# One attention-and-experts kernel: from hand-written loops to one list of small operations, with other load shapes for q, k and v

## The chip, the cores and the metric

The kernel runs on one core of a Trainium2 chip. The metric is the device time of one execution in microseconds (us), median over several runs. The core has five instruction queues that run side by side and meet only at semaphores: TensorE (PE, with weight loads shown as PEld), VectorE (DVE), ScalarE (ACT), GpSimd (POOL) and SyncE (SP, which here only issues DMA transfers). Each queue runs its instructions strictly in the order in which the program lists them.

## The reference, cut to what matters

```python
B, H, S, D = 8, 8, 576, 64            # batch, heads, tokens, head size
scores = q @ k.T / sqrt(D)            # per batch and head
scores = where(|i - j| <= 32, scores, -1e9)
x = softmax(scores) @ v               # -> 4608 tokens x 512
logits = x @ w_gate + modality_bias[modality_id]     # 8 experts
e = argmax(logits); g = max(softmax(logits))
out[token] = g * (relu(x[token] @ w1[e]) @ w2[e])    # w1 512x1024, w2 1024x512
```

Sliding-window attention gives one row of 512 values per token; each row goes to the one expert that its gate chooses.

## The kernel before

**Attention.** A batch has four pairs of heads, so there are 32 pairs (the loop variable `it`). q and k are loaded for four heads at a time with four tokens to a partition (packets of 1,024 bytes, `load_main`); the last 64 tokens of all heads come in a transfer of their own (`load_rest`, 256-byte packets), and v comes with one token to a partition (`load_v`, 256-byte packets). POOL casts all of it to bf16 (`pool_cast`, L110). PE transposes q and k (L212, L222), DVE and ACT copy the results out (L213, L214, L227, L225), PE makes scores of a 192-wide window (L238), ACT exponentiates (L242, L245), DVE multiplies by the band mask (L250), PE multiplies by v with a column of ones (L261, L266), and DVE divides (L271, L272).

**Routing.** After a batch's four pairs its rows are transposed (L349, L351) and multiplied by the gate (L360). Some 25 small DVE operations (`best`, `place`, `dispatch`) choose the expert and the row's place in a scratch table in DRAM; POOL scatters the rows there (L435).

**Experts.** The table is worked off in 19 tiles of 256 tokens. A tile is gathered by SP (L463), transposed (`turn`, L475 and L478), multiplied by w1 in four pieces (`up`, L490, relu on ACT at L492) and by w2 in two halves of two pieces each (`down`, L499), scaled on DVE (L503) and scattered to the output by POOL (L506). Two tiles per batch go to the two experts that are expected to be the fullest, with weights loaded once at the start (`load_ab`); the three tiles of `tail` may load other weights.

**What sets the order.** Two loops. The loop over `it` issues the stages of pairs `it`, `it+1` and `it+2`, loads of batch b+2 and casts of batch b+1. `trickle(n)` puts a few of the routing steps of the batch before into the gaps, `work(n)` a piece of a tile. After the last pair eight pairs' worth of loop steps are left, and `tail` follows. Nothing but this order decides what stands behind what in each queue. There is one PSUM buffer for `up` (tag "h"), one for `down` ("y"), one for scores ("s"), one for values ("o"), and two for all transposes ("tp").

Of the kernel before, what the change touches and what calls it, by code (L numbers as in the profile page):

```python
# [29 lines left out]

@with_exitstack
def kernel(
# [12 lines left out]
    nc = tc.nc  # L45
# [9 lines left out]
    R = 4  # L55
    SM = P * R
    SR = S - SM
# [18 lines left out]
    ld = ctx.enter_context(tc.tile_pool(name="ld", bufs=8))  # L76
    ldv = ctx.enter_context(tc.tile_pool(name="ldv", bufs=2))
    ldr = ctx.enter_context(tc.tile_pool(name="ldr", bufs=2))
# [15 lines left out]
    scr_ins = []  # L94

# [13 lines left out]
    def pool_cast(o_ap, i_ap):  # L109
        nc.gpsimd.tensor_scalar(out=o_ap, in0=i_ap, scalar1=1.0, scalar2=0.0, op0=ALU.mult, op1=ALU.add)  # L110


    Ld = {}

    def load_main(b, g):
        for u, src in ((0, q), (1, k)):
            f_ = ld.tile([P, 4, R * D], FP32, tag="qkf", name="qkf")
            nc.sync.dma_start(
                f_[:], src[b, 4 * g:4 * g + 4, 0:SM, :].rearrange("h (p r) d -> p h (r d)", r=R))
            Ld[b, g, u] = f_  # L120

    def load_rest(b):
        rf = ldr.tile([P, H, D], FP32, tag="rf", name="rf")
        nc.sync.dma_start(rf[0:SR], q[b, :, SM:S, :].rearrange("h s d -> s h d"))
        nc.sync.dma_start(rf[SR:P], k[b, :, SM:S, :].rearrange("h s d -> s h d"))
        Ld[b, "r"] = rf

    def load_v(b, eng):
        f_ = ldv.tile([P, NM - 1, H, D], FP32, tag="vf", name="vf")
        l_ = ldv.tile([SR, H, D], FP32, tag="vl", name="vl")  # L130
        for j in range(NM - 1):
            eng.dma_start(f_[:, j], v[b, :, P * j:P * j + P, :].rearrange("h s d -> s h d"))
        eng.dma_start(l_[:], v[b, :, SM:S, :].rearrange("h s d -> s h d"))
        Ld[b, "v"] = f_, l_
# [3 lines left out]
    def cast_main(b, g, split=False):  # L138
        for u in range(2):
            c_ = ldb.tile([P, R, 4 * D], BF16, tag=f"cb{u}", name="cb")  # L140
            o_ap = c_[:].rearrange("p r (h d) -> p h r d", h=4)
            i_ap = Ld[b, g, u][:].rearrange("p h (r d) -> p h r d", r=R)
            (nc.scalar.copy if split and u else pool_cast)(o_ap, i_ap)
            Ct[b, g, u] = c_

    def cast_rest(b):
        rb = ldr.tile([P, HD], BF16, tag="rb", name="rb")
        pool_cast(rb[:], Ld[b, "r"][:].rearrange("p h d -> p (h d)"))
        Ct[b, "r"] = rb

    def cast_v(b, i):
        f_, l_ = Ld[b, "v"]
        if i < 2:
            pool_cast(v_t[b % 2][:, 2 * i:2 * i + 2, :, 0:D].rearrange("p j h d -> p (j h) d"),
                      f_[:, 2 * i:2 * i + 2].rearrange("p j h d -> p (j h) d"))
        else:
            pool_cast(v_t[b % 2][0:SR, NM - 1, :, 0:D], l_[:])

    load_main(0, 0)
    load_rest(0)  # L160

    mb_bc = const.tile([P, n_mod, E], FP32)
    nc.scalar.dma_start(mb_bc[:], moe_modality_bias.partition_broadcast(P))
    mid64 = const.tile([NM * B, P], mybir.dt.int64)
    nc.vector.memset(mid64[:].bitcast(I32), 0)
    idv = moe_modality_id.rearrange("(b s) -> b s", s=S)
    for m in range(NM):
# [4 lines left out]
    load_v(0, nc.scalar)  # L172
    load_main(0, 1)
    ident = const.tile([P, P], BF16)
    make_identity(nc, ident[:])


# [9 lines left out]
    mask = const.tile([P, WIN], BF16)  # L187
    nc.gpsimd.memset(mask[:], 1.0)
    nc.gpsimd.affine_select(out=mask[:], in_=mask[:], compare_op=ALU.is_ge, fill=0.0,
                            base=0, pattern=[[1, WIN]], channel_multiplier=-1)  # L190
    nc.gpsimd.affine_select(out=mask[:], in_=mask[:], compare_op=ALU.is_ge, fill=0.0,
                            base=64, pattern=[[-1, WIN]], channel_multiplier=1)

    def prep(i):
        nc.vector.memset(q_t[i][:, :, 0:QP], 0.0)
        nc.vector.memset(q_t[i][:, :, QP + S:], 0.0)
        nc.vector.memset(k_t[i][:, :, S:], 0.0)
        pv = p_t[i][:].rearrange("p h (j c) -> p h j c", c=SW)
        nc.vector.memset(pv[:, :, :, WL:SW], 0.0)
        nc.vector.memset(v_t[i][:, 0:NM - 1, :, D:D + 1], 1.0)  # L200
        nc.vector.memset(v_t[i][0:SR, NM - 1, :, D:D + 1], 1.0)
        nc.vector.memset(v_t[i][SR:P, NM - 1], 0.0)
        nc.vector.memset(x_t[i][:, :, HD // 2 + 2:ROW // 2], 0)
    prep(0)
    cast_main(0, 0, split=True)
    cast_rest(0)


    def tr_rest(b):
        tpr = ps_t.tile([P, NH, P], BF16, tag="tp", name="tpr")  # L210
        for hp in range(NH):
            nc.tensor.transpose(tpr[:, hp, :], Ct[b, "r"][:, P * hp:P * hp + P], ident[:])  # L212
        nc.vector.tensor_copy(q_t[b % 2][:, :, QP + SM:QP + S], tpr[:, :, 0:SR])  # L213
        nc.vector.tensor_copy(k_t[b % 2][:, :, SM:S], tpr[:, :, SR:P])  # L214

    def tr_main(it):
        b, hp = divmod(it, NH)
        g, l = hp // 2, 2 * (hp % 2)
        for u in (1, 0):
            tp = ps_t.tile([P, R, P], BF16, tag="tp", name=f"tp{u}")  # L220
            for i in range(R):
                nc.tensor.transpose(tp[:, i, :], Ct[b, g, u][:, i, D * l:D * l + P], ident[:])  # L222
            i_ap = tp[:].rearrange("d r c -> d c r")
            if u:
                nc.scalar.copy(k_t[b % 2][:, hp, 0:SM].rearrange("d (c r) -> d c r", r=R), i_ap)  # L225
            else:
                nc.vector.tensor_copy(q_t[b % 2][:, hp, QP:QP + SM].rearrange("d (c r) -> d c r", r=R), i_ap)  # L227

    def scores(it, j0, st=None):
        b, hp = divmod(it, NH)  # L230
        pt = p_t[it % 2]
        if st is None:
            st = ps_s.tile([P, 2, 512], FP32, tag="s", name="st")
        for j in (j0, j0 + 1) + ((4,) if j0 else ()):
            c0 = WIN * (j - j0)
            w_ = WIN if j < NM - 1 else WL
            for h in range(2):
                nc.tensor.matmul(  # L238
                    st[:, h, c0:c0 + w_], k_t[b % 2][D * h:D * h + D, hp, P * j:P * j + P],
                    q_t[b % 2][D * h:D * h + D, hp, P * j:P * j + w_], start=True, stop=True)  # L240
        p_ap = pt[:, :, SW * j0:SW * j0 + 2 * SW].rearrange("p h (j c) -> p h j c", c=SW)[:, :, :, 0:WIN]
        nc.scalar.activation(  # L242
            p_ap, st[:, :, 0:2 * WIN].rearrange("p h (j c) -> p h j c", c=WIN), ACT.Exp, scale=scale)
        if j0:
            nc.scalar.activation(pt[:, :, 4 * SW:4 * SW + WL], st[:, :, 2 * WIN:2 * WIN + WL],  # L245
                                 ACT.Exp, scale=scale)

    def masking(it):
        p_ap = p_t[it % 2][:].rearrange("p h (j c) -> p (h j) c", c=SW)[:, :, 0:WIN]
        nc.vector.tensor_tensor(  # L250
            out=p_ap, in0=p_ap, in1=mask[:].unsqueeze(1).to_broadcast([P, 2 * NM, WIN]), op=ALU.mult)

    def values(it):
        b, hp = divmod(it, NH)
        pt, vt = p_t[it % 2], v_t[b % 2]
        xr = x_t[b % 2][:, :, 0:HD // 2].bitcast(BF16)
        ot = ps_o.tile([P, 2, 512], FP32, tag="o", name="ot")
        for h in range(2):
            for m in range(NM):
                o_ap = ot[:, h, (D + 1) * m:(D + 1) * (m + 1)]  # L260
                nc.tensor.matmul(  # L261
                    o_ap, pt[:, h, SW * m:SW * m + P], vt[:, m, 2 * hp + h, :],
                    start=(m == 0), stop=(m == 0), skip_group_check=True)
                if m > 0:
                    c1 = SW * (m - 1) + P
                    nc.tensor.matmul(  # L266
                        o_ap, pt[:, h, c1:c1 + P], vt[:, m - 1, 2 * hp + h, :],
                        start=False, stop=True, skip_group_check=True)
        o_v = ot[:, :, 0:NM * (D + 1)].rearrange("p h (m c) -> p h m c", c=D + 1)
        rec = small.tile([P, 2, NM], FP32, tag="rec", name="rec")  # L270
        nc.vector.reciprocal(rec[:].unsqueeze(3), o_v[:, :, :, D:D + 1])  # L271
        nc.vector.tensor_tensor(  # L272
            out=xr[:, :, P * hp:P * hp + P].rearrange("p m (h d) -> p h m d", h=2),
            in0=o_v[:, :, :, 0:D],
            in1=rec[:].unsqueeze(3).to_broadcast([P, 2, NM, D]), op=ALU.mult)

    cast_v(0, 0)
    cast_v(0, 1)
    cast_v(0, 2)
    load_main(1, 0)  # L280
    load_rest(1)
    load_main(1, 1)
    load_v(1, nc.sync)
    prep(1)


# [468 lines left out]
    def run_all(g):  # L755
        for _ in g:
            pass
# [133 lines left out]
```

## Time and profile before

| | us |
|---|---|
| median of 9 runs | 331.65 (330.55 to 333.26) |
| the profiled execution, as timed | 334.06 |
| its span, first to last instruction | 332.4 |
| values of the first pair divided (L271) | from 36.4 |
| of the 13th pair | from 110.6 |
| of the 32nd pair | from 236.1 |
| the last matmul ends | 315.7 |

Columns of a row of a window are the busy us of each engine in that stretch, with the number of instructions, the granted TensorE clock (1 is full), the mean load of the 16 DMA engines (packets of several queues overlap, so it can be over 1) and the rate. A row of a wait says who idled, which instruction ended it, the sum, how often and the longest. In a timeline the bracket at the end is the idle time before the instruction and what ended it.

### The profile page before, as it was taken

To read this page: it belongs to the slowest core of one execution; us is meant where nothing else is said; L and a number is where in the kernel's file an instruction comes from. 1 tells how busy PE (TensorE), PEld (TensorE's weight loads), DVE (VectorE), ACT (ScalarE), POOL (GpSimd) and SP (SyncE) were. 2 spreads that over 40 slices of the span, in tenths; PEclk is the share of its full clock that TensorE was granted. 3 is DMA by queue.
4 is the path that set the end of the run, shared out by engine and by line. 5 is a ranking of instruction groups with operands and counts; after the bars stand their busy time and mean duration, and the time that the engine had idled before them with its cause. 6 is when DMAs were issued, how large, how long until landed. Compare 5 with 4: busy or idle time off the path is not lost. (4 is left out here: it accounts for less than half of the span.)

```text
span 332.4 us, 6885 instructions
## 1 busy us (share of the span) xinstructions
PE 238.4 (72%) x2587; PEld 166.8 (50%) x2617; DVE 177.3 (53%) x464; ACT 162.3 (49%) x274; POOL 151.3 (46%) x195
## 2 busy tenths in 40 slices
PE   0104766736589989989988998998878799788700
PEld 0003554525466756756765675675655456555300
DVE  4025888833826587687789479657333741111100
ACT  0206575643437856857756765784544233343100
POOL 3159741286280636736837835814517312221310
PEclk9999997655569999999999999999999989999975
DMA  4999999999996952895597511231332764210110
GB/s 144 249 289 251 220 233 214 235 309 259 282 220 188 268 138 75 249 267 157 178 313 190 168 43 43 100 132 53 92 129 97 261 215 130 74 57 1 71 62 1
DMA packets 79351, 55.32 MB, mean 166 GB/s; under 512 B 49192, under 2 KB 74832, under 8 KB 79312
## 3 DMA queue, kind: packets, MB, share of 16 engines
q1 hardware_dynamic: 65504, 34.66, 42.0%
q0 software_dynamic: 8624, 18.66, 18.8%
q10 hardware_dynamic: 5184, 1.50, 2.2%
q8 instruction: 22, 0.36, 0.5%
q14 instruction: 17, 0.14, 0.1%
HBM read 54.64 MB, written 18.04 MB: 219 GB/s over the span
## 5 line engine op out<-in xcount | busy, mean ns | idle before, releaser
L490 PE MATMUL ph<-xTf,w 128*128 128x256 bf16 x608 | 81.7, 279 | 13.2 <-ACT xTf L478 6.6
L506 POOL DMA_INDIRECT out_dram<-ys,ix x38 | 38.0, 999 | 104.8 <-DVE ys L503 52.7
L499 PE MATMUL py<-w,hT 128*128 128x512 bf16 x274 | 74.8, 382 | 4.3 <-DVE ys L503 1.7
L492 ACT ACTIVATE hT<-ph 128x512 bf16<-128x512 f32 x76 | 45.3, 596 | 65.4 <-PE ph L490 64.3
L490 PEld LDWEIGHTS <-w 128*128 128x128 bf16 x608 | 58.2, 100 | 26.8 <-issue 10.9
L242 ACT ACTIVATE pt<-st 128x768 bf16<-128x768 f32 x64 | 51.7, 808 | 18.6 <-PE st L238 17.2
L503 DVE TENSOR_SCALAR ys<-py,xg 128x512 f32<-128x512 f32 x38 | 28.4, 747 | 51.4 <-PE py L499 51.4
L435 POOL DMA_INDIRECT scr<-xt,di x40 | 39.7, 992 | 21.5 <-issue 17.7
L222 PE MATMUL tp<-ident,cb 128*128 128x128 bf16 x256 | 25.9, 245 | 22.0 <-DVE kT L214 12.5
L250 DVE TENSOR_TENSOR pt<-pt,mask 128x1920 bf16<-128x1920 bf16 x32 | 40.1, 1253 | 2.4 <-ACT pt L245 2.4
L499 PEld LDWEIGHTS <-hT 128*128 128x128 bf16 x304 | 28.2, 98 | 25.2 <-issue 2.8
L110 POOL TENSOR_SCALAR cb<-qkf 128x1024 bf16<-128x1024 f32 x30 | 32.9, 1118 | 14.2 <-DMA qkf<-in_q_dram 4.7
L238 PE MATMUL st<-qT,kT 64*128 64x192 bf16 (+1 forms) x320 | 26.6, 267 | 8.9 <-DVE lo L363 3.5
L222 PEld LDWEIGHTS <-cb 128*128 128x128 bf16 x256 | 17.5, 108 | 29.9 <-DVE kT L214 14.0
L261 PE MATMUL ot<-vt,pt 128*128 128x65 bf16 x320 | 25.1, 205 | 7.1 <-POOL vt L110 6.2
L271 DVE RECIPROCAL rec<-ot 128x10 f32<-128x10 f32 x32 | 7.0, 218 | 42.9 <-PE ot L266 42.8
L227 DVE COPY qT<-tp 128x512 bf16<-128x512 bf16 x32 | 22.0, 686 | 13.5 <-PE tp L222 13.5
L272 DVE TENSOR_TENSOR xt<-ot,rec 128x640 bf16<-128x640 f32 x32 | 26.4, 824 | 2.5 <-DMA scr<-xt,di 1.4
L261 PEld LDWEIGHTS <-pt 128*128 128x128 bf16 x320 | 23.0, 105 | 7.9 <-DVE pt L250 1.9
L478 ACT COPY xTf<-tpf 128x1024 bf16<-128x1024 bf16 x19 | 19.2, 1012 | 13.1 <-PE tpf L475 13.1
L351 ACT COPY xTr<-tpx 128x512 bf16<-128x512 bf16 x40 | 21.8, 598 | 7.1 <-PE tpx L349 7.0
L225 ACT COPY kT<-tp 128x512 bf16<-128x512 bf16 x32 | 18.7, 584 | 13.1 <-POOL le L606 11.3
(143 smaller groups left out, 261.7 us busy)
## 6 DMA issues: line engine op xcount, KB each, us to landing
w<-in_moe_w_dram POOLq DMA_DIRECT2D x10, 1024.0 KB, 13.1
qkf<-in_q_dram SPq DMA_DIRECT2D x16, 512.0 KB, 7.6
qkf<-in_k_dram SPq DMA_DIRECT2D x16, 512.0 KB, 7.5
vf<-in_v_dram SPq DMA_DIRECT2D x28, 256.0 KB, 7.1
xg<-scr SPq DMA_DIRECT2D x19, 272.0 KB, 3.3
scr<-zero SPq DMA_DIRECT2D x8, 272.0 KB, 3.9
vf<-in_v_dram ACTq DMA_DIRECT2D x4, 256.0 KB, 3.4
rf<-in_q_dram SPq DMA_DIRECT2D x8, 128.0 KB, 6.7
```

The costliest lines, as they stand in the source:

```text
L110: nc.gpsimd.tensor_scalar(out=o_ap, in0=i_ap, scalar1=1.0, scalar2=0.0, op0=ALU.mult, op1=ALU.add)
L222: nc.tensor.transpose(tp[:, i, :], Ct[b, g, u][:, i, D * l:D * l + P], ident[:])
L238: nc.tensor.matmul(st[:, h, c0:c0 + w_], k_t[b % 2][D * h:D * h + D, hp, P * j:P * j + P], q_t[b % 2][D * h:D * h + D, hp, P * j:P * j + w ...
L242: nc.scalar.activation(p_ap, st[:, :, 0:2 * WIN].rearrange("p h (j c) -> p h j c", c=WIN), ACT.Exp, scale=scale)
L250: nc.vector.tensor_tensor(out=p_ap, in0=p_ap, in1=mask[:].unsqueeze(1).to_broadcast([P, 2 * NM, WIN]), op=ALU.mult)
L261: nc.tensor.matmul(o_ap, pt[:, h, SW * m:SW * m + P], vt[:, m, 2 * hp + h, :], start=(m == 0), stop=(m == 0), skip_group_check=True)
L435: ins = nc.gpsimd.indirect_dma_start(out=scr[:], out_offset=bass.IndirectOffsetOnAxis(ap=di[:, m:m + 1], axis=0), in_=xi[:, m, :], in_offs ...
L490: nc.tensor.matmul(ph[:, u, :], w1[:, kd, P * mi:P * mi + P], self.xT[:, kd, :], start=(kd == 0), stop=(kd == n_kd - 1))
L492: nc.scalar.activation(self.hT[:, 2 * mp:2 * mp + 2, :], ph[:], ACT.Relu)
L499: nc.tensor.matmul(self.py[:], self.hT[:, kf, P * s:P * s + P], w2[:, kf, :], start=(kf == 0), stop=(kf == n_kf - 1))
L503: nc.vector.tensor_scalar(out=ys[:], in0=self.py[:], scalar1=self.xg[:, s, HD // 2:HD // 2 + 1].bitcast(FP32), scalar2=None, op0=ALU.mult)
L506: ins = nc.gpsimd.indirect_dma_start(out=out, out_offset=bass.IndirectOffsetOnAxis(ap=self.ix[:, s:s + 1], axis=0), in_=ys[:], in_offset=N ...
```

## The change

The whole order is now a text, `ORDER`, of 1,270 names. Each name is one small function that issues one step for one index; a single loop at the end reads the text and calls them. Each engine's queue gets its steps in the order of the text. Upper-case letters are mostly PE (TQ and TK transposes of q and k, SA and SB scores, V values, X and L gate, R ranks, N, U and D transposes, up and down of a tile, Y the new reordering), lower-case ones the copies behind them with the engine after a slash (a is ACT, v is DVE, p is POOL).

```diff
-    R = 4; SM = P * R; SR = S - SM
+    R = 6; PR = S // R; SR = S % P               # 96 partitions, six tokens each
-    ld = tile_pool(name="ld", bufs=8)
+    ld = tile_pool(name="ld", bufs=6); ldw = tile_pool(name="ldw", bufs=1)
-    def load_rest(b): ...                        # last 64 tokens of q and k: gone
+    def l(_, b, g, u):                           # 1,536-byte packets
+        f_ = ld.tile([PR, 4, R * D], FP32, tag="qkf", name="qkf")
+        nc.sync.dma_start(f_[:], (q, k)[u][b, 4 * g:4 * g + 4].rearrange("h (p r) d -> p h (r d)", r=R))
+    def lv(_, b, j):
...
+        elif b in V_PERM:                        # batches 0 to 3: 1,024-byte packets
+            nc.sync.dma_start(Ct["lv", b][:].rearrange("p (h c) -> p h c", h=H),
+                              v[b, :, 0:4 * P, :].rearrange("h (p r) d -> p h (r d)", r=4))
+    def Y(_, b, j):                              # put these tokens in order again
+        yt = ps_t.tile([P, HD], FP32, tag="tp", name="yt")
+        for r in range(4):
+            nc.tensor.matmul(yt[:], perm[p0:p0 + 32, r, :],
+                             Ct["vb", b][p0:p0 + 32, r, :, :].rearrange("p h d -> p (h d)"),
+                             start=(r == 0), stop=(r == 3))
+    def yy(eng, b, j):
+        copy(eng, v_t[b % 2][:, j, :, 0:D], Ct["Y", b, j][:].rearrange("p (h d) -> p h d", h=H))
+    def turned(it, u):                           # six transposes of 96 columns, q or k
+        for i in range(R):
+            nc.tensor.transpose(tp[:, i, :], Ct["c", b, hp // 2, u][:, i, D * l_:D * l_ + P], ident[0:PR, 0:PR])
+    def turned_out(eng, it, u):                  # one copy of 128x576, on ACT or DVE
...
+    def U(bank, t, mp):                          # up: bank "h", or the scores' bank
+    def D_(bank, t, s, half):                    # down: bank "y", or the values' bank
...
+ORDER = """
+Kp0 lv0.0 Kb l0.1.0 lv0.4 l0.1.1 l1.0.0 l1.0.1 c0.0.0/p lv1.0 lv1.4 Kx Ka c0.0.1/a TQ0 l1.1.0 TQ1 Kc tq0/a
...
+y11.0 D11.1.0/o i14 u12.2 O11.0 U12.3/s D11.1.1 u12.3 N14 y11.1 U13.0 n14/a O11.1 F15 D12.0.0 u13.0 U13.1/s
...
+"""
+    for name, num, eng in re.findall(r"([A-Za-z]+)([\d.]*)(?:/(\w))?(?:\s|$)", ORDER):
+        op[name](eng, *[int(x_) for x_ in num.split(".") if x_])
```

Also: the gate's products have a bank of their own (they shared the scores' one); copies of x and of a tile's transposes are split between ACT and DVE; five of the smaller constant set-ups (`Ka` to `Kx`) stand where the text puts them; the number of tiles is read by all engines after the last step of the text and no longer before the first tile of `tail`. The amount of work of the experts, the routing and the scatters is the same.

## The prediction

> **What bounds the kernel now.** I read the page first, then cut the span at the first, 13th and last product with v and asked for the engines' busy time in each stretch.
>
> ```profile
> span 332.4 us, 6885 instructions
> PE 238.4 (72%) x2587; PEld 166.8 (50%) x2617; DVE 177.3 (53%) x464; ACT 162.3 (49%) x274; POOL 151.3 (46%) x195
> ...
> PEclk9999997655569999999999999999999989999975
> ```
>
> ```profile
> 0.00:36.10 36.10, 6.82 (x67) 4.89 (x67) 13.62 (x43) 8.45 (x12) 19.84 (x51) 1.00 1.07 231
> 36.10:110.30 74.20, 51.53 (x627) 37.44 (x627) 45.57 (x106) 40.70 (x72) 35.11 (x36) 0.72 1.04 240
> 110.30:235.80 125.50, 113.63 (x1421) 81.05 (x1437) 92.20 (x231) 84.92 (x149) 72.48 (x79) 1.00 0.54 157
> 235.80:315.70 79.90, 66.39 (x489) 43.42 (x494) 25.15 (x84) 28.22 (x44) 22.88 (x31) 0.98 0.34 113
> ```
>
> No engine is full over the span; each stretch has its own limit. In the first PE hardly works. In the second DMA is loaded (1.04) but no engine is. In the third PE is the fullest; in the fourth PE alone matters. Three views say why.
>
> Start, timeline of PE: the second transposes wait 9 us, since DVE's queue stands still behind constants that POOL makes only after v's casts, and these wait for v's transfer.
>
> ```profile
> 14.79 0.61 PE L212 MATMUL tpr<-ident,rb 128*128 128x128 bf16 x4 [14.79 <-POOL rb L110]
> 24.98 0.61 PE L222 MATMUL tp<-ident,cb 128*128 128x128 bf16 x4 [9.16 <-DVE kT L214]
> ```
>
> Second stretch, waits from 66 to 105: DVE waits for the values, these for v's cast, and that stands on POOL behind scatters whose addresses come from DVE. A loop of queues, not the transfer.
>
> ```profile
> DVE rec L271 <- PE ot L266: 16.4, 3, 8.4
> POOL scr L435 <- issue: 9.0, 9, 6.6
> ...
> PE ot L261 <- POOL vt L110: 6.2, 2, 6.0
> ```
>
> Last stretch, timeline of PE: pieces of a tile follow each other at 0.87 us, but each tile begins with a gap, because its transposes are copied out with nothing else to do.
>
> ```profile
> 273.20 0.61 PE L475 MATMUL tpf<-ident,xg 128*128 128x128 bf16 x8
> 274.96 1.03 PE L490 MATMUL ph<-xTf,w 128*128 128x256 bf16 x8 [1.16 <-ACT xTf L478]
> ```
>
> From the last matmul (315.7) to the end of the span 16.7 us pass.
>
> **The change, part by part**, against this execution (span 332.4, timed 334.06).
>
> *Start, 36.1 now.* The first transfer of q lands at about 7.2 (POOL's first cast starts at 7.23); 590 KB in place of 512 makes it about 8. The third transfer, v's 1 MB, waits in SP's queue for that landing as the third one does now (issued at 7.17), so with 1 MB per 4 us (the rate of 8 to 28 us) it lands near 13. POOL: the first cast has 1,536 elements a partition, 1.118 x 1.5 = 1.7 us, to 9.8; 5 us of constants; two casts of v (1.08 each), to 17. Then Y of batch 0, four groups of four matmuls of 512 columns. Column time at the start is 106 ns per 128, so 427 ns each, 6.8 us, to 24; the copy (as L492, 0.6), then V0 ends at about **25**. Gain 11. If the clock is full by then Y takes 3.5 and the gain is 14; if v lands 4 us late, 7.
>
> *Work from the first to the last V.* I counted the steps of the text on each engine and multiplied by the rows. DVE: 31 masks x 1.25, 31 divisions x 1.04, 24 q/k copies x 0.77 (0.686 for 512 columns, now 576), 12 x-copies x 0.69, 5 tile copies x 1.37, 13 scalings x 0.75, 3 Y copies x 0.75, 7 routings x 5.6, small rest 1.4: 157 by the rows. Rows overlap: all DVE rows before add up to 197 and cover 177.3, a factor 0.90, so **140**. POOL: 27 q/k casts x 1.68, 21 v-casts of 1.08 or 0.85, 34 scatters and 12 output scatters x 1.3 (0.99 and the gap of 0.30), rest 6: 132. ACT, same way: 128 by rows, 115 covered. PE at the full clock (spacings 56 ns per 128 columns, 109 per 256, 216 per 512; 29 per product with v): transposes 12 x 42 ns = 0.5 a pair, as now with its share of the rest; scores and values 0.9; ten tiles begun, eight up and seven down: **122**, of which Y is 12 x 0.86 = 10.
>
> So DVE becomes the fullest. Now there are 11 tiles done by the last V, in the list eight: work moves from here to the end, where only PE matters. How near to 140 can it come? The nearest row is the steady stretch, where a batch takes 26.6 us (13th to 29th pair, 110.6 to 217.1) and PE's columns in it, by the spacings below, add up to 22.2: the fullest queue reached 84%. I take **140 / 0.84 = 167** in place of 199.7, gain 33. Ends: 0.73 (DVE's own 92.2 of 125.5), 192; 0.95, 147.
>
> *Transfers.* From the DMA packets of the trace: 55 ns for 1,024 bytes, 21.5 for 256. A batch now: 2,048 x 55 + 5,632 x 21.5, over 16 engines 14.6 us. With 1,536 q/k packets, whose price lies between 69 (on the line to the 162 of a 4,096-byte packet) and 83 (by length), and 1,024 + 512 for v: 10.8 to 12.2. Weights add 23 us once. What V12 needs lands by 75, and it can't be reached by the engines before 85: cover enough, so nothing is counted. There are six buffers for q and k in place of eight: 1.5 batches of lead, not two.
>
> *After the last V, 79.9 now.* The text has 11 ups (3.49 each: 32 x 109 ns), 12 downs (3.46) and 9 transposes (0.45), with gate and ranks 1.9: **86** of PE. Up and down alternate between two banks, and each tile's transposes stand two pieces ahead, so that the 1.16 to 1.7 us gaps go. ACT has 37 and DVE 36 there: cover. The conditional weight loads cost 1.56 to 1.69 at two tiles now; they stay, 3 in all: **89**, 9 more than now. Next late: tile 12's gather, which stands behind the eight zero fills (8.6 us now) behind the routing of batch 7; it has about 2 us to spare; a loss of up to 5 is in the range.
>
> *End.* 16.7 and 0.5 for the tile count that PE now reads last (0.49 at L840): 17.
>
> Sum: 25 + 167 + 89 + 17 = 298; with the 1.7 around the span 299.7, against 334.06: 34.4 less. The median lies 2.4 under the profiled run, so 331.65 - 34.4 = **297**.
>
> **A rule against it.** The granted clock was 0.59 from 60 to 80 and 0.55 from 80 to 100, where PE was busy 10.75 and 14.11 of 20 us, and 1.00 from 100 on, with 19.01. The Trainium skill (TensorE: Matmul & The Clock Gate, "What's actually happening") says that the half clock is the default and about 3.4 us of steady work lift it. By it Y's matmuls fall where the clock is low: four batches 27.5 us and not 13.8. My sum hides them, since PE has 18 us to spare up to the last V.
>
> A second one: mask rows have a median of 1.148 and a longest of 2.189 us. The skill (SBUF — State Buffer, "Who interferes with whom") says that DVE with two SBUF inputs and a reading GpSimd block each other. By the rows this costs 0.1 a mask, already in the 1.25; longer casts could double it, 3 us.
>
> **Rivals.**
> - *Half clock up to V12.* PE has 48 us between V0 and V12 at the full clock, 95 at half, DVE's share of the 167 is 68: 27 more, 324. For it: the clock rows. Against: PE's work is denser, and from 40 to 53 us, at 3.5 us a pair, the clock was full.
> - *The list packs no better.* DVE stays at its 73% of the third stretch: 192 in place of 167, 322. For it: queues in order cannot adapt to a late transfer. Against: routing and casts are no longer put in by count.
> - *Denser.* 95% on DVE: 147, 277. For it: three engines have slack.
> - *Slower.* One mechanism: SP's single queue. Gathers stand in front of loads (F0 between v4's transfers, F4 and F5 in front of q6), and a gather waits for scatters; SP waited up to 19.6 for the addresses and 7.2 for the landing. The lead of a load is about eight pairs. If it shrank to three (3 x 5.4 = 16), the worst wait of 26.8 would leave 10.6 per batch, four batches 42: 339. It decides from 9 us per batch on. Against: F4 stands 9 pairs ahead of what it delays.
>
> **Numbers.** Forecast 55% (282 to 312), denser 15%, half clock 12%, no better packing 11%, the queue 5%, no change 2%. Eight in ten lie in 278 to 322. A measurement of this kernel tells about 0.3% from no change. Faster 0.93, same 0.02, slower 0.05.
>
> **What would show it.** V0 ends at 25, V12 at 85 to 95, the last V near 192; DVE about 80% busy between; tiles at the end every 7.6 to 8.0 us (now 9.3) with no gap in front of an up; clock full from V4. Wrong if PE waits for v or q casts for over 3 us at a time, if POOL idles "issue" in front of scatters, or if SP stands at a gather while POOL waits for a load.

## The result: 1.9% slower, and the profile after

The changed kernel took 344.72 us (median of ten runs, 337.0 to 348.74) beside 331.72 for the kernel before; the ratio is **1.019, interval 1.0145 to 1.0235**. The prediction was 297. Three of its ten runs lie at 337.0 to 338.7, seven at 343.0 to 348.7; the ratio is of the quicker ones, the profile that follows is one of the seven (346.25 us), and so the unedited kernel was run once more below (`e10_after_again`: 340.44, ratio 1.0258, interval 1.0165 to 1.0351; its profiled execution took 338.65). That profile is called the second execution below.

The page after, first part and granted clock:

```profile
span 344.6 us, 7134 instructions
PE 264.1 (77%) x2747; PEld 182.4 (53%) x2777; DVE 206.5 (60%) x466; ACT 164.2 (48%) x273; POOL 165.0 (48%) x191
...
PEclk9999999999996767679997899899999999999975
```

DVE was to do less (no rest loads, fewer copies out) and is busy 29 us longer than before (16 in the second execution, 193.6 us). Cut at the first, 13th and last product with v, as before; columns: span of the stretch, busy PE, PEld, DVE, ACT, POOL with counts, granted clock, DMA share, GB/s:

```profile
0.00:23.30 23.30, 9.99 (x89) 6.15 (x90) 14.64 (x51) 11.17 (x15) 13.67 (x36) 1.00 0.95 215
23.30:133.60 110.30, 78.97 (x780) 50.60 (x782) 68.81 (x128) 47.75 (x82) 53.71 (x60) 0.91 1.03 229
133.60:242.40 108.80, 90.12 (x1241) 67.07 (x1252) 91.44 (x189) 68.69 (x119) 65.24 (x58) 0.91 0.44 118
242.40:328.00 85.60, 84.97 (x649) 58.53 (x658) 30.89 (x99) 36.55 (x57) 31.10 (x39) 1.00 0.40 136
```

The first and the last row came as predicted. The second is the loss: 110 us in which no engine is 75% busy, with a DMA share of 1.03. Beside the second execution, whose spans add up stretch by stretch:

| stretch | before | predicted | unedited again | without casts on POOL (below) |
|---|---|---|---|---|
| to the first product | 36.1 | 25 | 23.3 | 25.7 |
| to the 13th | 74.2 | 65 (V12 at 90) | 108.9 | 97.3 |
| to the last | 125.5 | 102 | 101.9 | 98.0 |
| to PE's last matmul | 79.9 | 89 | 86.2 | 85.5 |
| to the end | 16.7 | 17 | 16.7 | 16.7 |
| span | 332.4 | 298 | 337.0 | 323.2 |

So the whole miss lies between the first and the 13th product. In the second execution the first eight products follow each other at 5.8 us a pair, near the 5.4 of the prediction (65 / 12); the loss sits in single steps, above all those to the ninth (23.1 us) and to the 13th (21.4). **Start.** PE's timeline shows the reorder waiting for v's cast for 1.05 us only, where 9 us went before:

```profile
16.31 1.90 PE L248 MATMUL yt<-vb,perm 32*128 32x512 bf16 x8 [1.05 <-POOL vb L185]
```

**The clock.** The granted clock is given as 1.00 up to 89 us (70 in the second execution), where its first entry in the trace stands. The spacing of the matmuls says otherwise. The same twelve transposes:

```profile
68.76 1.15 PE L447 MATMUL tp<-ident,cb 96*128 96x96 bf16 x12
...
135.94 0.68 PE L447 MATMUL tp<-ident,cb 96*128 96x96 bf16 x12
```

The products with v stand 55 ns apart in each of the first nine pairs (22 to 87 us), and 29 ns in the tenth and eleventh; both executions agree. So PE ran at half its speed up to the ninth product. In the kernel before the third to the fifth pair already had 29 ns.

**End.** A tile's pieces follow each other every 0.87 us and the next tile's transposes stand between them; the gap before an `up` is gone:

```profile
273.10 0.61 PE L730 MATMUL tpf<-ident,xg 128*128 128x128 bf16 x8
273.55 1.04 PE L751 MATMUL ph<-xTf,w 128*128 128x256 bf16 x8
274.42 1.03 PE L767 MATMUL py<-w,hT 128*128 128x512 bf16 x4
```

**The bad stretch.** Its waits from 60 to 110 (in total, times, longest):

```profile
POOL scr L629 <- issue: 27.2, 7, 25.4
PEld L503 <- DVE pt L489: 10.1, 2, 7.3
DVE ix L720 <- DMA xg<-scr: 9.3, 2, 7.8
...
PE ot L503 <- DVE pt L489: 8.9, 2, 6.4
...
PE tpf L730 <- DMA xg<-scr: 8.6, 1, 8.6
```

Two new waits: PE for the masks (L489), and DVE and PE for the first gather (13.0 us of PE in the second execution). The third, POOL's 25.4 at the scatters of batch 1, follows from the second in part: in DVE's queue the `i0` that waits for the gather stands in front of the routing of batch 1 (L567 and on), which makes those scatters' addresses; with the gather and `i0` moved (below) 16.6 us of it are left. One window shows the first wait whole:

```profile
60.65 0.98 POOL L629 DMA_INDIRECT scr<-xt,di  x1 [0.30 <-issue]
...
61.65 1.50 POOL L185 TENSOR_SCALAR cb<-qkf 96x1536 bf16<-96x1536 f32 x1
62.01 5.71 DVE L489 TENSOR_TENSOR pt<-pt,mask 128x1920 bf16<-128x1920 bf16 x1
63.09 0.64 POOL L185 TENSOR_SCALAR vt<-vl 64x512 bf16<-64x512 f32 x1
63.65 0.20 POOL L624 COPY xt<-ioi 128x5 int32<-128x5 int32 x1
63.80 2.91 POOL L185 TENSOR_SCALAR cb<-qkf 96x1536 bf16<-96x1536 f32 x2
...
67.78 0.29 PE L503 MATMUL ot<-vt,pt 128*128 128x65 bf16 x2 [6.40 <-DVE pt L489]
```

The mask starts under a cast and ends 1.01 us after POOL's last one (63.80 + 2.91 = 66.71): it did its work only when POOL was idle. Then PE goes on, 6.4 us late. In this execution 19 masks of 32 beside no cast took 1.15 us each; 13 beside casts took 3.02 in the mean (before: 14, 1.39). In the second execution 14 beside casts took 2.40; the longest there stands elsewhere, and PE goes on 4.33 us late:

```profile
102.91 6.62 DVE L489 TENSOR_TENSOR pt<-pt,mask 128x1920 bf16<-128x1920 bf16 x1
```

### The profile page after: what moved, and what is told of

It reads as the page before. It is cut to its first block, busy times and chain, and to the rows that moved or that the text cites. A ratio compares the mean times of both kernels' runs of the same rounds, so it can differ in the third digit from the quotient of the medians.

```text
span 344.6 us, 7134 instructions
## 1 busy us (share of the span) xinstructions
PE 264.1 (77%) x2747; PEld 182.4 (53%) x2777; DVE 206.5 (60%) x466; ACT 164.2 (48%) x273; POOL 165.0 (48%) x191
## 5 line engine op out<-in xcount | busy, mean ns | idle before, releaser
L489 DVE TENSOR_TENSOR pt<-pt,mask 128x1920 bf16<-128x1920 bf16 x32 | 61.1, 1909 | 5.5 <-ACT pt L478 5.4
L751 PE MATMUL ph<-xTf,w 128*128 128x256 bf16 x432 | 60.1, 286 | 0.9 <-ACT hT L757 0.9
L767 PE MATMUL py<-w,hT 128*128 128x512 bf16 x188 | 52.5, 397 | 1.6 <-issue 0.8
L185 POOL TENSOR_SCALAR cb<-qkf 96x1536 bf16<-96x1536 f32 x30 | 45.3, 1528 | 14.3 <-DMA qkf<-in_q_dram 8.2
L503 PE MATMUL ot<-vt,pt 128*128 128x65 bf16 x320 | 28.0, 216 | 23.6 <-DVE pt L489 23.2
L447 PE MATMUL tp<-ident,cb 96*128 96x96 bf16 x384 | 31.9, 241 | 12.7 <-POOL cb L185 10.1
L503 PEld LDWEIGHTS <-pt 128*128 128x128 bf16 x320 | 25.1, 112 | 30.2 <-DVE pt L489 26.6
L447 PEld LDWEIGHTS <-cb 96*128 96x128 bf16 x384 | 24.7, 117 | 20.1 <-POOL cb L185 10.3
L508 PE MATMUL ot<-vt,pt 128*128 128x65 bf16 x256 | 26.6, 216 | 0.0
L767 PE MATMUL pyo<-w,hT 128*128 128x512 bf16 x86 | 23.6, 379 | 0.5
L508 PEld LDWEIGHTS <-pt 128*128 128x128 bf16 x256 | 22.9, 113 | 0.0
L751 PE MATMUL phs<-xTf,w 128*128 128x256 bf16 x176 | 22.8, 273 | 0.0
```

The source lines that it names most:

```text
L447: nc.tensor.transpose(tp[:, i, :], Ct["c", b, hp // 2, u][:, i, D * l_:D * l_ + P], ident[0:PR, 0:PR])
L489: nc.vector.tensor_tensor(out=p_ap, in0=p_ap, in1=mask[:].unsqueeze(1).to_broadcast([P, 2 * NM, WIN]), op=ALU.mult)
L503: nc.tensor.matmul(o_ap, pt[:, h, SW * m:SW * m + P], vt[:, m, 2 * hp + h, :], start=(m == 0), stop=(m == 0), skip_group_check=True)
L508: nc.tensor.matmul(o_ap, pt[:, h, c1:c1 + P], vt[:, m - 1, 2 * hp + h, :], start=False, stop=True, skip_group_check=True)
L751: nc.tensor.matmul(ph[:, u, :], w1_sb[t % 2][:, kd, P * mi:P * mi + P], Ct["N", t][1][:, kd, :], start=(kd == 0), stop=(kd == n_kd - 1))
L767: nc.tensor.matmul(Ct["D", t, s], Ct["h", t][:, kf, P * s:P * s + P], w2_sb[t % 2][:, kf, :], start=(kf == 0), stop=(kf == n_kf - 1))
```

## The experiments

Kernels that are set side by side ran on one chip, with the kernel before beside them. That took 331 to 332 us on two of the chips and 348 to 353 on the three others, and so each ratio is to the kernel before on the same chip.

### The mask by itself

Three kernels hold only POOL operations and a mask on DVE. The first queues the mask under a burst of casts:

> The disputed cost by itself; the kernel computes nothing of the reference and writes zeros. DVE multiplies 128x1920 bf16 by the mask (two inputs in SBUF), three times each: alone, and queued so as to start while POOL runs 1, 2, 4 or 6 casts of 96x1536 back to back; with 4 and 6 casts also with a short memset of 128x128 behind each cast; and a one-input operation of the same size alone and against 4 casts. Theory of the shared port, burst form: alone 1.15 us; against a burst the mask lasts until the burst is over, so its length grows with the number of casts, about 1.5 us for each: over 4 us with four casts, over 7 with six, and no less with the memsets. Rival, turn by turn: the mask waits for one cast at most, 2.7 us whatever the number. Rival, bandwidth: the lengths grow by a small factor, under 2 us. One input: unchanged by the casts under each, or else the port is not what counts.

Measured: alone 1.09; under one to six casts 2.11 to 2.18; with memsets between them 2.11 to 2.18. One input: 0.60 alone, 1.62 to 1.69 under casts. So my theory fell: the mask waited for one cast, whatever the number, and the next cast then waited for the mask (2.37 in place of 1.47). But that leaves 5.71 unexplained. In the kernel (first profile), the six masks that outlasted a POOL operation all stood in a stretch of POOL that a DMA issue had opened. The second varies just that (q a cast of q, s a scatter):

```diff
-("second", "qqqqq", 1, 0)
+("scsecond", "sqqqq", 1, 0)
```

> Measures one operation by itself; nothing of the reference is computed and the output is zeros. In the first such measurement a mask that began under the first cast of a burst waited for that one cast only (2.11 to 2.18 us, any number of casts), while in the changed kernel masks stood for up to five POOL operations. Here the mask, in the kernel's own strided form, begins under the first, the second or the third of five casts, under casts in v's form, under mixed forms, behind a scatter that opens the burst, and beside copies on ACT. Theory turn by turn: 2.2 us at most in all. Theory that a burst under way keeps the port: 2.2 under the first cast, over 5 us under the second or third. Theory that the scatter's descriptors make POOL keep the port: over 5 us only behind a scatter. Theory of mixed forms: over 3 us only there.

Five casts, the mask beginning under the second; then a scatter and four casts, the mask beginning behind the scatter:

```profile
68.93 8.30 POOL L77 TENSOR_SCALAR cast<-src 96x1536 bf16<-96x1536 f32 x5 [4.30 <-DVE cast L94]
...
70.51 1.09 DVE L121 TENSOR_TENSOR xsecond<-xsecond,mask 128x1920 bf16<-128x1920 bf16 x1
...
232.80 1.52 POOL L87 DMA_INDIRECT scr<-xs,rows  x1 [3.91 <-DVE xs L98]
...
234.25 6.88 DVE L121 TENSOR_TENSOR xscsecond<-xscsecond,mask 128x1920 bf16<-128x1920 bf16 x1
234.35 5.77 POOL L77 TENSOR_SCALAR cast<-src 96x1536 bf16<-96x1536 f32 x4
```

Without a scatter, in every position and form: 1.09 to 2.06 us. Behind a scatter: 6.88, 4.64 (beginning one cast later), 6.35 and 5.89 (casts of v's form); each ends 1.0 us after the whole burst. **Casts directly behind a DMA issue of POOL keep DVE out for several casts, here to the end of the burst.** In the kernel two of the six masks got in ahead of the last cast of their burst, a short one of v (64x512, which then took about 1.5 us and not 0.6). The third asks what frees it:

> One operation by itself; nothing of the reference is computed, the output is zeros. Behind a scatter the mask stood until POOL's burst was over (6.9 us), without a scatter for one cast at most. Here: scatter and four casts again (6.9 expected); a memset on POOL between scatter and casts (6 if it frees nothing, 2.2 if it does); an ordinary DMA issued by POOL in place of the scatter (2.2 if only descriptors that POOL writes itself count, over 6 if any issue does); POOL made to wait on DVE between scatter and casts (2.2 if a wait frees the port, over 4 if the scatter counts however long ago); a one-input operation behind a scatter (0.6 if only two inputs count, over 5 if any DVE access to that port does); a memset between the casts as well (over 5, as in the kernel with such memsets).

The mask behind scatter and memset, behind an ordinary DMA, and behind a scatter after which POOL had to wait for DVE (and then filled a small tile):

```profile
54.04 2.22 DVE L140 TENSOR_TENSOR xmemset<-xmemset,mask 128x1920 bf16<-128x1920 bf16 x1
...
74.08 6.01 DVE L140 TENSOR_TENSOR xdirect<-xdirect,mask 128x1920 bf16<-128x1920 bf16 x1
...
99.26 1.09 DVE L140 TENSOR_TENSOR xwait<-xwait,mask 128x1920 bf16<-128x1920 bf16 x1
```

Both kinds of DMA that were tried do it, not the scatter alone. One memset between the issue and the casts frees the port; with a wait ahead of that memset the mask, which begins as the first cast ends, gets in ahead of the second (a wait by itself was not run); a memset between the casts as well holds it again (3.79 with two casts). A one-input operation is held too: 5.88 for 0.60. Which of POOL's steps decides stays open.

### Casts taken off POOL

In the kernel, first k's 15 casts to ACT, then those of q too, then all but the first four of the start (29 of q and k and 7 of v to ACT, 14 of v to DVE). Four names, which stand apart in the text, as an example of the last:

```diff
-c1.0.0/p c1.0.1/p cw1.0/p cw1.1/p
+c1.0.0/a c1.0.1/a cw1.0/a cw1.1/v
```

> Edit of the changed kernel: the 14 casts of k that stand on POOL go to ACT at the same places of the list. Port theory (DVE's masks, which read two SBUF operands, are kept out while POOL runs casts back to back): bursts of casts get half as long, the 32 masks fall from 61 us in all to 45 to 50 and the whole kernel gets 10 to 20 us faster, although ACT gets 22 us more work. Gather theory (DVE and PE stand at the first two gathers, which are late in SP's queue): masks may fall, the time changes by less than 5 us. Reorder theory (the four groups of matmuls that put v in order cost the time): within 2 us.

Measured: 332.75, ratio 1.0025 (0.9984 to 1.0067); masks 52.5 us in sum, last product at 225.8. By the ratios that is 5 to 8 us less than the unedited kernel (1.019 and 1.0258), not the 10 to 20 expected, and the masks are longer than expected.

> All casts of q and k on ACT, those of v stay on POOL. Theory of the shared port: POOL is left with v's casts of under 1.1 us, so the masks sum up to 38 to 43 us (52.5 with only k's casts moved, 61.1 before that), and the time falls under the 332.7 of that kernel, to 322 to 330. Theory of the late gather alone: the casts are no part of it; the step of the ninth pair stays at 17 us and the time at 332 to 338. Rival, ACT becomes the bound: 14 casts of 1.47 are 20 us more on ACT, of which PE waits for the exponentials; 336 to 345.

Measured: masks 38.9, as expected, but 362.38, ratio 1.0283 (1.0186 to 1.038), on a chip where the kernel before takes 353.1. That is no gain against the ratio of the unedited kernel; what part of it the chip has is not known, since the unedited kernel did not run there.

> The changed kernel unedited, beside the two that follow, on one chip: 1.02 to 1.04 of the kernel before, masks 60 us in sum, 13th pair at 130 to 135 us, last pair near 240.

> All casts but the first four of the start leave POOL: q's, k's and half of v's for ACT, the other half for DVE; the gathers stay where the change has them. Theory of the shared port: no mask over 1.3 us, 37 us in sum; although DVE gets 12 casts more, the middle shrinks by more than with k's casts alone, 15 to 25 us below the unedited kernel. Theory of the late gather: 5 at most, since the ninth pair still waits 17 us. Rival, ACT becomes the bound: no gain over the unedited kernel although the masks are at 37.

Side by side on one chip: unedited 340.44 (1.0258), no casts on POOL **326.44, ratio 0.9863 (0.981 to 0.9916)**: 13 us less by the two ratios (14.0 by the medians), somewhat under the 15 to 25 expected, and faster than the kernel before. The masks' row (busy, mean ns) of the unedited kernel, from the first profile (54.2 us in sum on this chip):

```profile
L489 DVE TENSOR_TENSOR pt<-pt,mask 128x1920 bf16<-128x1920 bf16 x32 | 61.1, 1909 | 5.5 <-ACT pt L478 5.4
```

The same row without casts on POOL, each mask now at the length it has alone:

```profile
L489 DVE TENSOR_TENSOR pt<-pt,mask 128x1920 bf16<-128x1920 bf16 x32 | 37.0, 1157 | 8.8 <-ACT pt L478 8.4
```

PE's waits for masks from 24 to 235 us, unedited and then without casts on POOL, fall by 10.3 us, most of what was gained. That the masks and not some other wait behind POOL's casts made the difference rests on these two rows:

```profile
PE ot L503 <- DVE pt L489: 12.6, 6, 4.3
...
PE ot L503 <- DVE pt L489: 2.3, 2, 1.8
```

The two stretches of the middle, unedited again, columns as above:

```profile
23.30:132.20 108.90, 76.47 (x786) 49.62 (x787) 60.28 (x129) 47.85 (x82) 54.11 (x60) 0.86 1.03 232
132.20:234.10 101.90, 87.66 (x1235) 64.93 (x1247) 87.20 (x190) 68.70 (x119) 66.64 (x58) 0.95 0.48 127
```

And without casts on POOL:

```profile
25.70:123.00 97.30, 69.65 (x786) 46.01 (x787) 53.87 (x137) 67.35 (x100) 17.66 (x30) 0.82 1.05 236
123.00:221.00 98.00, 85.32 (x1235) 64.49 (x1246) 75.03 (x196) 88.70 (x138) 34.27 (x35) 0.98 0.56 149
```

Of the 13.8 us of span, 11.6 come before the 13th product, 3.9 from there to the last and 0.7 behind it, less 2.4 at the start. In the second stretch ACT is now 91% and PE 87% busy: it is packed. The first stays loose, with DMA at 1.05 and PE at half its speed for most of the way: 55 ns between the products of eight of the first nine pairs (29 in the sixth), and half by the clock's own entries from 54.2 to 88.3.

> The kernel without casts on POOL again, on the chip of the run before: 0.98 to 0.99 of the kernel before on a chip where that takes 331 us; masks 37 us in sum, 1,536-byte packets at 104 to 112 ns.

Measured on another chip: 362.32, ratio 1.0413 (1.0346 to 1.048), with the kernel before at 347.9. So this version beats both kernels on a chip where the kernel before takes 331 us, and loses to the kernel before on this one, where the unedited kernel did not run. Masks again 36.9. What its trace shows more there are stops that it puts down to no engine:

```profile
ACT hT L757 <- remote: 16.1, 4, 5.5
```

All eight traces of the changed kernel's versions from such chips have them, up to 5.8 us long; none of those from the quicker chips has. The kernel before has no profile on such a chip; why they punish the list more stays open.

A memset of 128x128 behind each cast, to let the mask in:

> Edit of the changed kernel: POOL fills a small tile (128 x 128 fp32, about 0.2 us, reads nothing) behind each of its casts: 50 more instructions, about 10 us more work for POOL. Port theory: DVE gets in between two casts, no mask is longer than 1.15 plus one cast (2.7 us), the masks fall to about 45 us and the kernel gets 5 to 15 us faster in spite of the added work. Gather theory and reorder theory: slower by 0 to 5 us.

Measured: 345.0, ratio 1.0307 (1.0226 to 1.0387), masks 56.5, the longest 5.86. No gain, as the last measurement by itself would have told.

### The first gather

```diff
-l3.0.1 l3.1.0 F0 F1
+F0 F1 l3.0.1 l3.1.0
```

(`F0`, `F1` directly behind the last scatter of batch 0, `i0`, `i1` later on DVE.)

> Edit of the changed kernel: the first two gathers stand right behind the scatters that they wait for, in front of the loads of the second and third q/k tiles of batch 3, and DVE's two index steps that read them stand in front of the first scaling. Gather theory: DVE's 9.3 us and PE's 8.6 us of waiting for the gather go to under 2, and the time falls by 8 to 15 us. Port theory: these waits go as well, but the masks stay at 58 to 62 us and the time falls by less than 5 us, as the next long mask takes their place. Reorder theory: within 2 us.

Measured: 336.25, ratio 1.0126 (1.0082 to 1.0171); the ninth product at 77.9 in place of 86 to 87, its step 9.0 us in place of 17.4 to 23.1, and PE's wait for the gather gone. Beside the second execution the lead of 9 us at the ninth product is 6 at the 13th (125.8 and 132.2) and 1 at the last (232.9 and 234.1). The masks stay long, 60.2 us, and the time falls by under 5 us, both as the theory of the port had it: against 1.019 and 1.0258 for the unedited kernel that is 0.6 to 1.3%, 2 to 4 us, with intervals that overlap.

> k's casts on ACT and the first two gathers put ahead of four loads. If the stretched masks and the late gather are two costs that stand one behind the other, their gains add: 332.7 less 5 to 10, 322 to 328, with the ninth pair's step at 9 us and the masks at 50 us. If they are one cost seen twice (POOL's burst also delays the scatters that the gather waits for), nothing is added: 330 to 333.

> All casts of q and k on ACT and the gathers early. Port and gather as two costs: 312 to 322, below the kernel before (331.7) and the clock at full more of the time. If ACT takes the place of DVE as the engine that is waited for: 325 to 335. If a third cause sets the middle (the order of PE's pieces, in which 13th pair stands behind routing and four groups of reordering): the step to the 13th pair stays at 20 us and the time above 325.

> The same with the first two gathers ahead of four loads. If port and gather are the two causes and add, this is 25 to 35 us below the unedited kernel and 0.93 to 0.97 of the kernel before. If a third cause holds the middle (PE's half clock through the first tiles and the reordering of v): the last pair stays later than 220 us and the ratio at 0.99 or above.

Measured, the first two on a chip with the kernel before at 353.1: with k's casts on ACT 356.51, 1.0076 (1.0021 to 1.0131); with q's and k's 355.63 to 353.14, a quotient of 1.007 without an interval; without casts on POOL 327.53, 0.9893 (0.9838 to 0.9949), no better than 326.44 without the early gather.

The last two answers differ. Without casts on POOL the ninth product comes at 79.5 and not 87.2, but the 13th at 125.3 and not 123.0: the gain of the gather is used up by then. With q's and k's casts on ACT the run without the early gather stood on the same chip (362.38): all its runs lie at 361.4 to 364.5, those with the early gather at 351.3 to 358.2, 6.8 us less by the medians, and here the lead is kept, 7.6 us at the ninth product, 8.9 at the 13th (123.0 and 131.9) and 9.8 at the last (245.9 and 255.7). So port and gather added up in one pair of runs and not in the other, and why is open. The last pair at 223.2 and 0.9893 in the run without casts is close to what its expectation gave to a third cause, PE's half clock and the reordering of v; no run changed the clock by itself.

### v without the reorder

`V_PERM` empty, all batches of v in 256-byte packets, no Y:

> Edit of the changed kernel: v of all batches loaded one token to a partition in 256-byte packets, its casts straight to where they are used at the places of the old ones, and no reordering on TensorE (64 matmuls and 16 copies less). Reorder theory: 10 to 20 us faster. Port theory: the casts stay on POOL, masks stay at 55 to 62 us; the time goes by the added packet time (about 2 us of 16 engines per batch, four batches) and by the matmuls that go: within 6 us either way. Gather theory: the gathers stand behind more and smaller packets and land later, slower by up to 5.

Measured: 345.2, ratio 1.0401 (1.0356 to 1.0446). No gain from leaving out the reorder. But the edit brings smaller packets with it, and the gather comes later still, so that what the reorder costs by itself is not shown:

```profile
DVE ix L719 <- DMA xg<-scr: 20.7, 3, 17.7
```

### Transfers

`W0` and `W1` (4 MB of weights) behind the scatters of batch 0, without casts on POOL, then with the early gather, then alone:

```diff
-W0 sa1 l2.0.1
+sa1 l2.0.1
...
-B0.3 W1 SA6
+B0.3 SA6
...
-Z0.4 yy2.3/a
+Z0.4 W0 W1 yy2.3/a
```

> On top of the kernel without casts on POOL (326.4 us, middle 25.7 to 221.0): the first two experts' weights, 4 MB as they land, are fetched behind the scatters of batch 0 and not at 18.7 to 22. Up to 88 us the DMA engines are full (share 1.13) while no engine is, and SP's issues stand for up to 11 us. If the transfers set this stretch, the loads of batches 1 to 3 come some 15 to 20 us sooner, the ninth pair ends near 75 in place of 87, and the time falls by 5 to 12. If the gather's place in SP's queue sets it, the ninth pair moves by 3 at most. Rival: the weights then come late for the first tile and the time is given back or grows by up to 10.

> The same with the first two gathers ahead of four loads. Transfers and gather as one cause (the gather is late because SP's issues stand in full queues): as the run before, within 3 us. As two causes: 5 to 10 us less than that run, the 13th pair before 112. Rival, weights late for the first tile: PE waits for them once over 5 us.

> The changed kernel with its casts on POOL, only the weights late. If the transfers cost the middle by themselves: 5 to 12 us below the unedited kernel's 340. If the port and the bursts behind scatters hold everything: within 3 us of it, masks still 54 to 61 us in sum.

Measured: ratios 1.0426 (1.0361 to 1.0492), 1.028 (1.0204 to 1.0355) and 1.0583 (1.0515 to 1.0651) on a chip with the kernel before at 349.3. All three lose to the kernel before. None of the kernels that they edit ran on this chip; the nearest is the one without casts at 1.0413 (1.0346 to 1.048) on another chip of that kind, the same as the first within the noise and 1.3% above the second, with intervals that just overlap. So what late weights are worth is not settled. In the first the ninth product comes at 93.8, later and not sooner, and PE's longest wait for the gather is 13.2 us in place of 7.8. In the second (the profiled execution took 369.99 us, the shortest 358.23) the ninth comes at 75.1, the earliest of all, and the 13th at 137.2: what is won ahead of it is lost behind it. In the third the masks sum up to 49.6, below the 54 to 61 expected.

Each q and k load in two transfers of 1,024 and 512 bytes a packet:

```diff
-        nc.sync.dma_start(f_[:], s_)
+        nc.sync.dma_start(f_[:, :, 0:4 * D], s_[:, :, 0:4 * D])
+        nc.sync.dma_start(f_[:, :, 4 * D:R * D], s_[:, :, 4 * D:R * D])
```

> The kernel without casts on POOL, with each load of q and k in two transfers, of 1,024 and of 512 bytes a packet, in place of one of 1,536. In the traces 1,024 bytes took 55 ns, 256 took 22, and 1,536 took 104 to 112 where the prediction had 69 to 83. If the price grows with 1,024-byte pieces, the two packets take 55 and about 33, 88 for 108, 1.9 us less of 16 engines a batch; if transfers hold the stretch up to the 13th pair, that pair comes 5 to 8 us sooner and the time falls by 3 to 8. If they are cover enough, as the prediction had it: within 2 us of the kernel beside it. If the price is per packet whatever its size, the transfers grow and the time with them, by 3 to 8.

Measured: 363.79 beside 362.32, no difference that counts. Up to 25 us a packet of 1,536 takes 110 ns in the one; in the other one of 512 takes 40, and the 1,024-byte packets of q and k about 73 (mean of all 66, v's 56 taken out): 113 together. The price goes by bytes, not by packets, and lies some 30% above that of v's 1,024-byte packets (110 / 1.5 = 73 against 56 ns per 1,024 bytes).

## Why the prediction was wrong, point by point

- **Start, 25: right** (23.3), in part by luck: at half clock the four groups of Y were to take 6.8 us one behind the other, but they ran in pairs side by side (single matmuls of the trace begin at 16.31 and 16.32, 16.69 and 16.72, and so on) and took 1.90 a pair. **After the last V, 89: right** (86.2). **End, 17: right.** V12 to the last V, 192 - 90 = 102: right in the second execution (101.9; 108.8 in the first), although by chance in part: without casts on POOL it took 98.0, so some 4 us of it go with the casts, and the rest packed better than expected.
- **The failed step is "140 / 0.84 = 167" for the work from the first to the last V**, which took 211 to 219. It spread one packing rate over a stretch that has two parts, and so gave the first twelve pairs 65 us; they took 109. The 84% came from the steady stretch, where DMA is at half load and one engine is nearly full. In the first part no engine sets the pace: loads, the first gather, routing and POOL's scatters wait for one another through queues in order. The table of before had it: 74 us there, DMA 1.04, no engine over 70%. Nor was DVE the fullest engine: it was busy 147.5 us in the second execution, near the 140, but PE, put at 122 ("at the full clock"), was busy 164.1, of which 76.5 up to the 13th product where the prediction had 48. (Busy time counts somewhat more than the spacings that the 122 was made from.)
- **"Longer casts could double it, 3 us" was mis-sized**: masks grew by 14 to 21 us of DVE in sum (40.1 to 54.2 and 61.1), and taking the casts off POOL gave 13 us on a chip where the kernel before takes 331. The prediction reckoned with longer casts; what counts is that the list puts several of them directly behind a DMA issue of POOL while a mask is due.
- **"10.8 to 12.2 us" a batch of transfers was mis-sized**; whether "cover enough, so nothing is counted" fell with it is not shown. Measured, 1,536-byte packets took 105 to 109 ns in the stretches of after, not 69 to 83: 1,536 x 105 + 1,024 x 56 + 512 x 23 over 16 engines is 14.4 us a batch, the 14.6 of before; 16.7 with v in 256-byte packets. The Trainium skill (SBUF — State Buffer, "Door 1: The DMA port swizzle") says that the bandwidth of a transfer depends on how many of 16 ports its partitions reach; by its map 96 partitions reach all 16, eight ports with eight partitions and eight with four. It does not say what uneven ports cost. If the fullest port set the time, 96 partitions would take what 128 do, 55 x 1.5 x 128/96 = 110 ns a packet, an estimate that the trace comes near; no run here changed the number of partitions alone.
- Rivals. *SP's single queue* named the right queue and sign, but the other way round: the loads held the first gather (issued at 72 to 73 us, behind one issue of 10 us and five more), not the gather the loads; and it was one wait (PE 7.8 to 13.0 us), not one in each batch. Moving it brought 2 to 4 us back, 6.8 in one pair of runs and nothing in another. *Half clock up to V12*, given 12%, fits better than its share: PE ran at half its speed up to the ninth product, and "clock full from V4" failed. Its price of 27 us is not shown. PE was busy 41.4 us there in the second execution, so that at the full clock it would have been busy about 21 us less; that is an estimate of the most that PE itself lost, since PE also waited. *Packs no better*: half right, for the first part only.
- Of the signs that would make it wrong one came true: POOL idled "issue" in front of the scatters for 25.4 us. Between the first and the 13th product SP did not stand at a gather, and PE waited for casts for 2.2 us at most.

**What stays open.** Without casts on POOL the middle is 195.3 and not 167, so 28 of the 44 us (211 less 167) have no cause that a run shows. Split loads changed nothing, early gathers helped in one pair of runs and not in another, and late weights had no kernel beside them. Two causes are argued and not shown. The transfers: a share of 1.05 over the stretch up to the 13th product, but 0.72 from 95 to 105 us of it, and no run made them less. PE's half clock up to the ninth product: no run changed it alone, and the waits may be its cause as well as its effect.

## What to carry to other kernels

Before predicting a reordered list, cut the span where the load changes kind and give each part its own limit; a packing rate holds only in the part it was read from. Where DVE reads two tiles in SBUF, keep POOL's casts from standing directly behind a DMA that POOL issues (not tried in the kernel), or give them to another engine (a gain of 13 us on one chip; on the slower chips none is shown). Price a transfer from rows of the same shape, not only the same packet size. Hold the clock column against the spacing of the matmuls before relying on it.

## What the runs showed of the hardware

- The Trainium skill (SBUF — State Buffer, "Who interferes with whom") says that whoever issues first gets the shared port pair for the whole instruction and the other is blocked. The casts alone agree: a mask waits for one cast at most (2.18 us in all). Behind a DMA issue of POOL the trace differs: four casts in a row went first (6.88), so the measurement goes beyond the rule.
- A memset directly behind the issue frees the port (2.22); with a second one between the casts the mask is held again (3.79), and memsets behind each cast in the kernel leave a longest mask of 5.86.
- An issue of a DMA on SP can be long: with the DMA share at 1.1, one of 128 KB of v in 256-byte packets held SP for 9.99 us, and the first gather stood behind it.
- Packets to 96 partitions moved 14 to 15 bytes per ns (1,536 in 105 to 109), those of v to 128 moved 18 (1,024 in 56).
- The clock column can miss the start: it gives 1.00 where transposes and products stand twice as far apart (1.15 us for 0.68, 55 ns for 29).
